# A hand-searched order of a quad's work, replaced by two orders in turn, with one more stretch in which GpSimd gets no weight steps

## Chip, cores and metric

The kernel runs on one core of a Trainium2 chip. The metric is device time in microseconds (us). Three runs of the kernel before gave 2235.53, 2234.50 and 2234.67 us, median 2234.67 us. A difference is told in us and as a share of that median.

## What is computed

A transformer block over x of 2048 tokens by 576 features, in float32: a layer norm with scale and shift, attention with 32 query heads of width 18 and one shared key and value head, the output projection added to x, a second layer norm pair, and an MLP of width 4608 with GELU, added to x.

```python
mod = (_silu(c) @ w_mod).reshape(c.shape[0], 6, 1, -1)
sa, ca, ga, sb, cb, gb = (mod[:, 0], mod[:, 1], mod[:, 2], mod[:, 3], mod[:, 4], mod[:, 5])
h = _layernorm(x, axis=-1) * (1 + ca) + sa
x = x + ga * _A_ref(h, A_wq, A_wk, A_wv, A_wo)      # 32 heads, one key/value head
h = _layernorm(x, axis=-1) * (1 + cb) + sb
x = x + gb * _B_ref(h, B_w1, B_b1, B_w2, B_b2)      # layer norm, dense, GELU, dense
```

In the attention each query row has the maximum of its scores subtracted ahead of the exponential, so every score is computed twice: once, queries by keys, to find the maximum, and once, keys by queries, for the exponential.

## The kernel before

Time falls into three parts: projections (to about 128 us), 32 "quads" of attention (to about 1380 us), and the MLP. A **quad** is four heads for one block of 512 tokens; 8 quads make a block (`NQ`), 32 all (`NQT`). The program order is written by hand: every engine takes its instructions in the order in which the code issues them, and a helper adds the waits.

What a quad does is written as a list of short words (`order`, lines 884 to 893), which the loop at lines 980 to 1021 turns into instructions:

- `S0`, `S1` (`st_mm`, matmul L931): one score tile, 128 keys by 512 queries, into a `psB` bank of PSUM, by the upper or the lower 64 rows of TensorE (the digit); ScalarE (ACT) takes the exponential of it into `P` (L933). 64 a quad.
- `M0`, `M1` (`mx_mm`, matmul L319): one score tile, queries by keys, of the **next** quad into a `psM` bank; VectorE (DVE) takes its row maximum (L953). 48 a quad.
- `X1` and `R1`: the same for a folded pair of key blocks: `X1` is a matmul (L941) into `psB` and a Relu on ACT (L944) into `xc`, `R1` a matmul into `psM` and a fused add and maximum on DVE (L951). 8 of each.
- `V2` to `V4` (`pv_mm`, L921): so many quarters of a step P times V, into the one `psC` bank, eight quarters behind the scores. A quad has 64 quarters; a step of four is called kc, 0 to 15.
- `T1`, `RC`, `T2`, `OS`: the steps of `post_quad` (L738 to L758) for the quad before: its first step, a copy of `psC` to `O` on ACT, is issued when its last P times V is; then `T1` a transpose on DVE (L741), `RC` a reciprocal on DVE (L744) and behind it a product on GpSimd (POOL, L745), `T2` the transpose back on DVE (L747), `OS` a rounded copy `os` of `O` on ACT (L757), a difference on POOL (L758) and four DMAs on SP's queue.
- `F1`, `F2`: the maxima of the next quad are put together on DVE, turned by TensorE (PE, L357), split on ACT and DVE and sent by DMA into its query tile.
- `WO` (`wo_piece`, L723): 14 matmuls of the output projection into one `psB` bank, and the addition to x on DVE (L727). There are 24 such pieces; from quad 9 on, each quad has one.

`psM` has three banks, `psB` four, `psC` one. So PE can stand at most three tiles ahead of DVE and four ahead of ACT; when it meets a word whose bank is not free, all words behind it wait as well.

Three things ride along. Every second `WO` piece finishes a tile of 128 tokens, and its second layer norm (`ln2_tile`) is then issued step by step, one step at every second kc (`between`): statistics on DVE (L143, L147, L148), rows on POOL, and at the end five transposes by PE, a copy `yr` on ACT (L165) and one on DVE (L167), which are held back until the next `WO` (`held`). Weight steps (`prep`, a generator: `weight_parts`) prepare the MLP's weights on POOL and store them by SP's queue: from quad 4 on one or two of them at each kc but those in `quiet`, which before were the two kc ahead of the `F2` word. What is left of them is issued at kc 8 of quad 31. And `load_q` loads a query tile per quad.

Quads 0 to 8 use the list `QUAD`; quads 9 to 30, which hold an output piece, used `QUADW`; quad 31 has its own.

Of the kernel before, what the change touches and what calls it, by code (L numbers as in the profile page):

```python
# [19 lines left out]
NQ = H // 4  # L20
# [12 lines left out]
def block_kernel(ctx: ExitStack, tc, x, wqkv, wo, w1, b1, w2, b2, c, wmod, ident_in, out):  # L33
# [50 lines left out]
    V = pa.tile([128, S // 128, 32], F32, name="V")  # L84
# [409 lines left out]
    WO, YR, ATT, B2 = {}, {}, {}, {}  # L494
# [283 lines left out]
    def load_w1(i, what):  # L778
        for w in what.split():
            a = 4 * OPS.index(w) if w in OPS else 28  # L780
            b = min(a + 4, 31)
            sy.dma_start(W1["r"][:, a:b].bitcast(F32), w1scr[i, :, a:b])
# [86 lines left out]
    def tail_parts(o, tail, d, e=po):  # L869

        e.tensor_tensor(d, tail[:, 0], tail[:, 1], op=ALU.subtract)
        for x, y in ((o[:, :2], tail), (o[:, 2], d)):
# [11 lines left out]
    QUAD = """S0 M0 S1 S1 M0 V3 S0 M1 S1 M0 M1 S0 V3 M0 S1 M1 S0 V2 M0 S1 S1 M0 X1 S0 V4 T1 X1 M0 M1 M0 S1 S0  # L884
# [1 line left out]
            M1 V3 M0 S1 S1 M0 S0 R1 S0 V3 R1 S0 S1 M1 S0 M0 X1 V3 M0 S1 M0 S1 S0 S0 R1 V3 M0 X1 S0 M1 S0 M1  # L886
            V3 S1 M0 M0 S1 T2 S0 S1 V4 M0 S1 S0 M1 S0 M1 V3 S0 R1 S1 M0 F1 S1 S0 V3 X1 M0 S1 M0 R1 S0 F2 OS
            V4 M0 M1 S0 S1 M0 X1 V4 S1 M0 S1 S0 M1 M0 S1 V2 R1 S0 M1 S0 V2 S0 S1 M0 M1 V2 S1""".split()
    QUADW = """S0 M1 S0 S1 M0 S1 V4 M0 S1 M0 S1 S0 M1 V4 X1 M0 M1 S0 T1 X1 S0 V4 S0 M1 M0 S1 M0 S1 V4 S1 S0 RC
            R1 M0 S1 S0 R1 V4 S1 M0 S1 S0 M0 X1 M0 V3 S0 M1 S1 M0 S1 M0 S1 V3 S0 M1 S0 X1 M0 T2 OS V2 M0 R1  # L890
            S0 S1 S0 M1 WO X1 M0 S1 M0 R1 S0 V4 S1 M0 S1 M0 S1 M0 S1 V3 M1 S0 S0 M1 S0 S1 M0 V3 S0 M1 R1 S0
            S1 M0 V3 S0 M1 M1 S0 X1 S0 V3 M1 M0 S0 S1 R1 S0 V4 M0 S1 M0 F1 S0 S1 M0 S1 V4 F2 S1 M0 X1 M0 S1
            M0 V2 S1 S0 M1 S0 V2 M1 S0 S1 M0 V2 M0 S1 M0 S1 S1 S0 M1 V3 M0 X1 S0 R1 S0 R1 V3""".split()
    LASTW = "S0 S1 S0 S1 S0 S1 WO V4 S0 S1 V4".split()
    LAST = "S0 S1 S0 S1 V4 S0 S1 S0 S1 V4".split()
    P, PVt = {}, {}
# [17 lines left out]
    def pv_mm(n, kc, h0, h1):  # L914

        if kc == 0 and h0 == 0:
            PVt[n] = psC()
        t = P.pop((n, kc)) if h1 == 4 else P[n, kc]
        cs = slice(128 * h0, 128 * h1)
        for j in range(4):  # L920
            pe.matmul(PVt[n][32 * j:32 * (j + 1), cs], V[:, kc, :], t[:, j, cs],  # L921
                      start=(kc == 0 and h0 == 0), stop=(kc == 15), skip_group_check=True)
        if kc == 15 and h1 == 4:
            posts.append(post_quad(n, PVt.pop(n)))
            next(posts[0])

    def st_mm(n, kc, g, i, ps):
        if (n, kc) not in P:
            P[n, kc] = pb.tile([128, 4, TB], F32, name="P", bufs=4)
        t = ps()  # L930
        pe.matmul(t, KS[64 * g:64 * g + 64, 128 * kc:128 * (kc + 1)], QST[n][64 * g:64 * g + 64, i, :],  # L931
                  start=True, stop=True)
        ac.activation(P[n, kc][:, 2 * i + g, :], t, AF.Exp, scale=SCALE)  # L933
# [3 lines left out]
    def mx_mm(n, u, kb, what, g):  # L937
        p, qt = UNITS[u]
        if what == "X":
            t = psB()  # L940
            pe.matmul(t, QST[n][64 * g:64 * g + 64, p, 128 * qt:128 * (qt + 1)], KD1[64 * g:64 * g + 64, :],  # L941
                      start=True, stop=True)
            XC.append(pb.tile([128, 512], F32, name="xc", bufs=2))
            ac.activation(XC[-1], t, AF.Relu)  # L944
            return
        t = psM()
        o = mx_tile(n)[:, 8 * g + 4 * p + qt, (2 if what == "R" else kb):][:, :1]
        smax_mm(n, t, g, p, qt, 3 if what == "R" else kb)
        if what == "R":
            c = XC.popleft()  # L950
            ve.tensor_tensor_reduce(c, t, c, 1.0, -3.0e38, ALU.add, ALU.max, o)  # L951
        else:
            ve.tensor_reduce(o, t, axis=AX.X, op=ALU.max)  # L953

    def between(n, kc):

        if kc == 1 and n >= 1 and n + 2 < NQT:
            load_q(n + 2)
        if kc % 2 and (held[0] != "T" or not pieces):
            held[0] = step(fill)  # L960
        if n > 3 and kc not in quiet:
            for _ in range(1 + (kc % 4 != 3)):
                step(prep)
        if kc == 8 and n == NQT - 1:
            while prep:
                step(prep)
# [3 lines left out]
    def wo_next(ps):  # L970
        tb, t, h2 = pieces.popleft()
        wo_piece(tb, t, h2, ps())
        for _ in range(2):
            if held[0] == "T":
                held[0] = step(fill)
        if h2 and tb < 2:
            fill.append(ln2_rows(tb, t))

    pq = 0
    for n in range(NQT):  # L980
        ns = [0, 0]
        if n < NQT - 1:
            order = QUADW if n > NQ else QUAD
            if n == NQT - 2:
                order = order + ["WO"]
        else:
            order = []
            for d in range(8):
                order += LASTW + ["RW"] if d == 4 else LAST
                order += {1: ["T1"], 2: ["RC"], 4: ["T2"], 5: ["OS", "V4"]}.get(d, [])  # L990
        if n < NQT - 1:
            kc = sum(int(tok[1]) for tok in order[:order.index("F2")] if tok[0] == "V") // 4
            quiet = kc - 2, kc - 1
        for tok in order:
            if tok[0] == "V":
                g = int(tok[1])
                while g:
                    i = min(g, 4 - pq % 4)
                    if pq >= LAG:
                        pv_mm(*divmod((pq - LAG) // 4, 16), pq % 4, pq % 4 + i)  # L1000
                    pq, g = pq + i, g - i
                    if pq % 4 == 0:
                        between(*divmod(pq // 4 - 1, 16))
            elif tok[0] == "S":
                g = int(tok[1])
                st_mm(n, ns[g] // 2, g, ns[g] % 2, psM if ns[g] % 2 and (n == NQT - 1 or n == NQT - 2 and ns[g] > 24) else psB)
                ns[g] += 1
            elif tok in maxima:
                unit = next(maxima[tok], None)
                if unit:  # L1010
                    mx_mm(*unit, tok[0], int(tok[1]))
            elif tok == "WO":
                wo_next(psB)
            elif tok == "RW":
                for i, w in enumerate("hl"):
                    sy.dma_start(WO[w][:, KD - 1, :].bitcast(F32), woscr[i])
            elif tok[0] == "F":
                (smax_fin1 if tok == "F1" else smax_fin2)(n + 1)
            elif n:
                if next(posts[0], 0) == 0:  # L1020
                    posts.pop()
        if n == NQT - 1:
            W1["r"] = per.tile([128, 40, 128], F32R, name="w1a", tag="big", bufs=3)
            load_w1(0, " ".join(OPS) + " tails")
# [480 lines left out]
```

## Time and profile before

| what | value |
|---|---|
| median of three runs | 2234.67 us |
| the profiled execution's own time | 2233.75 us |
| its span from first to last instruction | 2232.0 us |
| so outside the span | 1.75 us |
| busy: PE, DVE, ACT, POOL | 2206.7, 1936.0, 1645.7, 1529.3 us |
| from quad 9's second kc to the start of quad 30 | 508.11 to 1304.12 us |

The profile is of one execution. An engine's busy time is the union of its instructions' times; an instruction whose start is earlier than its forerunner's end overlaps it, so that 48 reduces of 682 ns each take 30.5 us together. Where a row ends in square brackets, the engine stood idle for that long ahead of it, and the name is what it waited for last. A quad's start is taken here as the start of its first exponential. Line numbers are those of the kernel before; in the changed kernel, lines from 894 on stand five further down.

### The profile page before, as it was taken

How to read it: one execution, taken by the hardware profiler on the slowest of the kernel's cores; microseconds unless marked ns; L12 is line 12 of the kernel's file. 1: busy time of each engine (PE TensorE's matmuls, PEld its weight loads, DVE VectorE, ACT ScalarE, POOL GpSimd, SP SyncE). 2: the span in 40 equal slices, each digit the busy share in tenths (PEclk: the TensorE clock that was granted, in tenths of full speed). 3: DMA queues.
4: the chain of work that ended last, by engine and by line, in shares of the span. 5: the costliest groups of instructions: out<-in, count | busy, mean ns of one | idle time of the engine just before them, and what ended most of it. 6: DMA issues, size and time to landing. Idle time of an engine off the chain costs nothing.

```text
span 2232.0 us, 45861 instructions
## 1 busy us (share of the span) xinstructions
PE 2206.7 (99%) x16454; PEld 1437.8 (64%) x16454; DVE 1936.0 (87%) x3415; ACT 1645.7 (74%) x3145; POOL 1529.3 (69%) x1761
## 2 busy tenths in 40 slices
PE   7999999999999999999999999999999999999999
PEld 5654444444444445444454445888888898988898
DVE  7589999999999999999999982887888878888887
ACT  5579999999999999999999997444444544343443
POOL 6653456777877787778776200888888867877776
PEclk9999999999999999999999999999999999999999
DMA  6232143443433333333333101655665646676563
GB/s 232 84 129 92 34 138 121 150 135 116 145 118 123 124 135 112 124 132 121 129 124 128 44 13 60 200 179 176 180 179 175 189 126 182 182 216 189 177 185 123
DMA packets 184776, 307.99 MB, mean 138 GB/s; under 512 B 19711, under 2 KB 75407, under 8 KB 184549
## 3 DMA queue, kind: packets, MB, share of 16 engines
q1 hardware_dynamic: 184405, 304.91, 43.0%
q8 instruction: 130, 2.13, 0.4%
q14 instruction: 97, 0.79, 0.1%
q10 hardware_dynamic: 144, 0.15, 0.0%
HBM read 200.97 MB, written 93.79 MB: 132 GB/s over the span
## 4 chain that ended last, share of the span: by engine, by line
PE 88%; DVE 3%; ACT 3%; issue 1%; POOL 0%; ACTq 0%; POOLq 0%; DVEq 0%
PE psC L921 22%; PE psB L1144 18%; PE psA L1247 16%; PE psB L931 14%; PE psM L319 11%; PE psB L723 2%; ACT P L933 2%; PE psB L941 2%; PE psA L1281 1%; DVE mx L953 1%; PE psA L723 1%; DVE xc L951 1%; PE psB L155 0%; PE psB L357 0%; PE psB L248 0%
## 5 line engine op out<-in xcount | busy, mean ns | idle before, releaser
L933 ACT ACTIVATE P<-psB 128x512 f32<-128x512 f32 x2008 | 1043.6, 617 | 32.3 <-PE psM L319 10.4
L953 DVE TENSOR_REDUCE mx<-psM 128x1 f32<-128x512 f32 x1476 | 938.2, 683 | 36.2 <-PE psM L319 16.5
L319 PE MATMUL psM<-KS,qst 64*128 64x512 f32 x1722 | 601.8, 442 | 0.3 <-DVE mx L337 0.2
L931 PE MATMUL psB<-qst,KS 64*128 64x512 f32 x2008 | 586.0, 430 | 0.3 <-ACT P L933 0.2
L921 PE MATMUL psC<-P,V 128*32 128x256 f32 (+3 forms) x6424 | 575.8, 448 | 0.5 <-ACT O L738 0.5
L931 PEld LDWEIGHTS psB<-qst,KS 64*128 64x128 f32 x2008 | 303.9, 185 | 216.0 <-ACT P L933 140.4
L1144 PE MATMUL psB<-ops,w1a 128*128 128x512 f32 x1512 | 393.9, 396 | 0.2 <-DVE h L1159 0.2
L319 PEld LDWEIGHTS psM<-KS,qst 64*128 64x128 f32 x1722 | 275.6, 184 | 163.2 <-DVE mx L953 121.3
L1144 PEld LDWEIGHTS psB<-ops,w1a 128*128 128x128 f32 x1512 | 270.2, 188 | 46.8 <-DVE h L1159 0.6
L921 PEld LDWEIGHTS psC<-P,V 128*32 128x32 f32 x6424 | 140.2, 108 | 200.5 <-issue 173.3
L1253 DVE TENSOR_TENSOR XT<-psA,XT 128x576 f32<-128x576 f32 x330 | 241.8, 753 | 18.5 <-PE psA L1247 13.2
L1247 PEld LDWEIGHTS psA<-w2s,big 128*128 128x128 f32 x1584 | 223.0, 188 | 14.0 <-POOL big L1221 2.5
L1247 PE MATMUL psA<-w2s,big 128*128 128x288 f32 x1584 | 230.5, 294 | 0.0
L1157 ACT ACTIVATE psB<-gs 128x512 f32<-128x512 f32 x144 | 86.7, 602 | 127.8 <-DVE gs L1156 127.8
L1221 POOL TENSOR_TENSOR big<-s,big 128x512 fp32r<-128x512 f32 x132 | 171.1, 1296 | 10.6
L1153 ACT ACTIVATE h<-psB,b1t 128x512 f32<-128x512 f32 x144 | 98.1, 681 | 102.4 <-PE psB L1144 81.4
L951 DVE CUSTOM_DVE_ANT_0 xc<-psM,xc 128x512 f32<-128x512 f32 x246 | 165.9, 681 | 4.2 <-PE psM L319 1.9
L758 POOL TENSOR_TENSOR os<-O,os 128x512 fp32r<-128x512 f32 x31 | 40.0, 1289 | 172.2 <-ACT os L757 172.2
L944 ACT ACTIVATE xc<-psB 128x512 f32<-128x512 f32 x246 | 152.4, 620 | 5.1 <-PE psM L319 2.7
L1156 DVE SCALAR_TENSOR_TENSOR gs<-psB,h 128x512 f32<-128x512 f32 x144 | 98.6, 684 | 39.9 <-ACT psB L1154 39.8
L792 POOL TENSOR_TENSOR r<-r,r 128x256 fp32r<-128x256 f32 (+1 forms) x162 | 122.1, 754 | 13.0
L1162 ACT ACTIVATE big<-h 128x512 fp32r<-128x512 f32 x39 | 24.7, 634 | 133.8 <-DVE h L1159 133.8
(212 smaller groups left out, 3326.7 us busy)
## 6 DMA issues: line engine op xcount, KB each, us to landing
w1a<-w1scr SPq DMA_DIRECT2D x252, 256.0 KB
w2s<-w2sum SPq DMA_DIRECT2D x132, 288.0 KB
w1scr<-r SPq DMA_DIRECT2D x126, 256.0 KB
w2s<-w2scr SPq DMA_DIRECT2D x76, 288.0 KB
w2scr<-r SPq DMA_DIRECT2D x72, 288.0 KB
w2sum<-r SPq DMA_DIRECT2D x72, 288.0 KB
qst<-qscr SPq DMA_DIRECT2D x192, 72.0 KB
w1a<-w2scr SPq DMA_DIRECT2D x33, 288.0 KB
```

Of the source, the lines that this page charges most:

```text
L319: pe.matmul(o, QST[n][64 * g:64 * g + 64, p, 128 * qt:128 * (qt + 1)], KS[64 * g:64 * g + 64, 512 * kb:512 * (kb + 1)], start=True, stop=True)
L792: po.tensor_tensor(o[:, n:2 * n], src, o[:, :n].bitcast(F32), op=ALU.subtract)
L921: pe.matmul(PVt[n][32 * j:32 * (j + 1), cs], V[:, kc, :], t[:, j, cs], start=(kc == 0 and h0 == 0), stop=(kc == 15), skip_group_check=True)
L931: pe.matmul(t, KS[64 * g:64 * g + 64, 128 * kc:128 * (kc + 1)], QST[n][64 * g:64 * g + 64, i, :], start=True, stop=True)
L933: ac.activation(P[n, kc][:, 2 * i + g, :], t, AF.Exp, scale=SCALE)
L944: ac.activation(XC[-1], t, AF.Relu)
L951: ve.tensor_tensor_reduce(c, t, c, 1.0, -3.0e38, ALU.add, ALU.max, o)
L953: ve.tensor_reduce(o, t, axis=AX.X, op=ALU.max)
L1144: pe.matmul(o, x, y, start=(first and i == 0), stop=(i == len(terms) - 1), skip_group_check=True)
L1221: po.tensor_tensor(unit(u, 1), x, unit(u, 0).bitcast(F32), op=ALU.subtract)
L1247: pe.matmul(p[:, i, :288], x[:, ts_], W2S[k][:, y], start=(bool(first) and q == 0), stop=(q == 2), skip_group_check=True)
L1253: ve.tensor_tensor(o, p[:, :, :288], o, op=ALU.add)
```

## The change

`QUADW` gets new words in a new order, and a second list `QUADV` of the same kind is added. Quads 10, 12 to 30 use `QUADV`, quads 9, 11 to 29 the new `QUADW`. Both hold the same work as the list before, in 19 runs of P times V in the place of 20. `quiet` gets a third kc, the one ahead of `RC`, in all quads from 4 to 30; the two ahead of `F2` stay as a rule. Of the lists only their first lines are shown.

```diff
-    QUADW = """S0 M1 S0 S1 M0 S1 V4 M0 S1 M0 S1 S0 M1 V4 X1 M0 M1 S0 T1 X1 S0 V4 S0 M1 M0 S1 M0 S1 V4 S1 S0 RC
...
+    QUADV = """M1 M0 S1 S0 M0 S1 S1 V4 M0 X1 M0 S1 S0 M1 V4 R1 S0 S1 S0 M1 S0 V4 T1 M1 M0 S1 S0 M1 S0 V4 S1 RC
...
+    QUADW = """M0 S1 S0 M1 S0 S1 M0 V4 M1 S0 S1 S0 M1 M0 V4 M0 S1 M1 S0 S1 S0 V4 T1 S0 M1 S0 M1 M0 S1 V2 M0 S1
...
-            order = QUADW if n > NQ else QUAD
+            order = (QUADW if n % 2 else QUADV) if n > NQ else QUAD
...
-            kc = sum(int(tok[1]) for tok in order[:order.index("F2")] if tok[0] == "V") // 4
-            quiet = kc - 2, kc - 1
+            kf, kr = (sum(int(tok[1]) for tok in order[:order.index(a)] if tok[0] == "V") // 4 for a in ("F2", "RC"))
+            quiet = kf - 2, kf - 1, kr - 1
```

Three places show what moves. The first is ACT in quad 20 (a `QUADV` quad after the change) from ahead of the output piece to behind it; `os` is the copy of the attention output, `yr` the copy of the norm's transposes, which stand right behind the output piece. Before:

```order
L944 ACTIVATE xc<-psB 128x512
L757 ACTIVATE os<-O 128x512
L933 ACTIVATE P<-psB 128x512 x3
L165 ACTIVATE yr<-psB 128x4x128
L944 ACTIVATE xc<-psB 128x512
```

and of the change:

```order
L949 ACTIVATE xc<-psB 128x512 x2
L938 ACTIVATE P<-psB 128x512 x5
L757 ACTIVATE os<-O 128x512
L938 ACTIVATE P<-psB 128x512
L165 ACTIVATE yr<-psB 128x4x128
```

`os` has moved to the other side of two exponentials: one exponential instead of three stands between it and the piece.

The second place is DVE at the same piece; L727 is the addition of the piece to x, L747 the transpose `T2`, which `os` reads. Before:

```order
L953 TENSOR_REDUCE mx_13550<-psM 128x1 x8
L747 STREAM_TRANSPOSE O<-T 128x512
L953 TENSOR_REDUCE mx_13550<-psM 128x1
L951 ISA xc,mx_13550<-psM,xc 128x512
L951 ISA mx_13550 128x1
L953 TENSOR_REDUCE mx_13550<-psM 128x1
L727 TENSOR_TENSOR XT<-psB,XT 128x288
```

and of the change:

```order
L958 TENSOR_REDUCE mx_13558<-psM 128x1
L747 STREAM_TRANSPOSE O<-T 128x512
L956 ISA xc,mx_13558<-psM,xc 128x512
L956 ISA mx_13558 128x1
L958 TENSOR_REDUCE mx_13558<-psM 128x1
L727 TENSOR_TENSOR XT<-psB,XT 128x288
```

Two tiles instead of three now stand between the transpose and the addition.

The third place is ACT in quad 21 (a new `QUADW` quad) and the start of quad 22. Before, `os` stood ahead of the piece here too. Of the change, from the split of the maxima (`ms`) on:

```order
L359 ACTIVATE ms<-psB 16x128
L938 ACTIVATE P<-psB 128x512 x10
L757 ACTIVATE os<-O 128x512
L938 ACTIVATE P<-psB 128x512 x8
L949 ACTIVATE xc<-psB 128x512
L938 ACTIVATE P<-psB 128x512 x2
L738 ACTIVATE O<-psC 128x512
```

`os` has moved from the middle of the quad to its last run of words, eleven tiles ahead of the copy that writes `O` anew.

More of the change, by code (lines that the diff above doesn't have):

```diff
@@ L888, in block_kernel @@
             V4 M0 M1 S0 S1 M0 X1 V4 S1 M0 S1 S0 M1 M0 S1 V2 R1 S0 M1 S0 V2 S0 S1 M0 M1 V2 S1""".split()
-    QUADW = """S0 M1 S0 S1 M0 S1 V4 M0 S1 M0 S1 S0 M1 V4 X1 M0 M1 S0 T1 X1 S0 V4 S0 M1 M0 S1 M0 S1 V4 S1 S0 RC
[L890 to L893, printed above, removed]
+    QUADV = """M1 M0 S1 S0 M0 S1 S1 V4 M0 X1 M0 S1 S0 M1 V4 R1 S0 S1 S0 M1 S0 V4 T1 M1 M0 S1 S0 M1 S0 V4 S1 RC
+            M0 S0 S1 M0 M0 X1 V3 M1 S0 S1 S0 R1 X1 M0 V3 S1 M0 S0 S1 M1 S0 R1 V3 M0 S1 S1 S0 M0 M0 X1 V3 M1
+            X1 S0 S1 M0 R1 S0 V4 M0 S1 T2 S0 R1 OS M0 S1 WO S1 M0 M1 S0 M0 S1 S0 V3 M0 S1 M1 S1 S0 M0 X1 V3
+            M0 S1 S0 S0 R1 M0 S1 V4 M1 S0 M1 S0 S1 M0 V2 S1 M0 S1 S0 V2 S0 F1 M1 S0 M1 S1 M0 V4 F2 S0 S1 M0
+            M1 S0 M1 V4 S1 M0 S1 S0 X1 M0 V4 M0 S1 X1 M0 S0 R1 V3 M0 S1 S0 S0 R1 S1 M0 V3""".split()
+    QUADW = """M0 S1 S0 M1 S0 S1 M0 V4 M1 S0 S1 S0 M1 M0 V4 M0 S1 M1 S0 S1 S0 V4 T1 S0 M1 S0 M1 M0 S1 V2 M0 S1
+            X1 M0 S1 V3 M0 S1 M0 S1 S0 R1 X1 V3 S0 M1 S1 M0 S1 S1 M0 V3 R1 M0 S1 S0 X1 M0 X1 V4 RC S1 S0 R1
+            M0 R1 S0 WO S0 M1 M0 M0 S1 S0 X1 V3 S0 M1 S1 R1 S0 M0 X1 V3 M0 S1 S0 S0 M1 R1 S0 V3 M0 S1 S0 S0
+            M1 M0 S1 V2 M0 S1 X1 M0 V2 M1 S0 M0 S1 S0 X1 M0 V4 S1 F1 M0 S1 S0 R1 S0 M1 V4 T2 F2 S1 M0 S1 M0
+            M1 S0 V4 S0 S1 M0 S1 S0 M1 V4 S1 M0 S0 R1 S1 M0 V4 OS M0 S1 M0 S1 S0 M1 S0 V4""".split()
     LASTW = "S0 S1 S0 S1 S0 S1 WO V4 S0 S1 V4".split()
```

## Prediction

> **What bounds the kernel now.** First the page: the span, the busy shares, the slices of DVE and ACT, and the chain that ended last.
>
> ```profile
> span 2232.0 us, 45861 instructions
> PE 2206.7 (99%) x16454; PEld 1437.8 (64%) x16454; DVE 1936.0 (87%) x3415; ACT 1645.7 (74%) x3145; POOL 1529.3 (69%) x1761
> DVE  7589999999999999999999982887888878888887
> ACT  5579999999999999999999997444444544343443
> PE 88%; DVE 3%; ACT 3%; issue 1%; POOL 0%; ACTq 0%; POOLq 0%; DVEq 0%
> ```
>
> By the page PE is busy 99% and holds the chain. But the page says itself that matmul ends are modelled, and in slices 4 to 23, the quads, DVE and ACT stand at nine tenths as well. So the next view is the busy time of each engine in single quads: 5 (no output piece), 11, 20 and 21 (output piece and norm), and 29 (output piece, the norm is over).
>
> ```profile
> core 0: us, PE busy (x) PEld busy (x) DVE busy (x) ACT busy (x) POOL busy (x), PEclk, DMA share, GB/s
> 319.03:356.38 37.35, 37.35 (x365) 18.48 (x365) 36.51 (x71) 36.97 (x76) 26.83 (x40) 1.00 0.42 141
> 588.40:629.07 40.67, 40.31 (x348) 19.54 (x349) 38.80 (x78) 38.62 (x78) 31.00 (x43) 1.00 0.34 113
> 907.44:947.59 40.15, 39.79 (x342) 19.32 (x341) 38.28 (x76) 38.13 (x76) 30.57 (x42) 1.00 0.30 102
> 947.59:987.18 39.59, 39.50 (x337) 18.67 (x336) 37.93 (x75) 37.56 (x76) 31.76 (x46) 1.00 0.42 138
> 1264.99:1304.10 39.11, 39.02 (x337) 18.64 (x337) 37.27 (x72) 37.51 (x75) 3.02 (x3) 1.00 0.07 20
> ```
>
> Subtract the busy time from the length. In quad 5 DVE is idle 0.84 us and ACT 0.38: that order runs at the speed of ACT. In quad 20 DVE is idle 1.87 and ACT 2.02, in 21 it is 1.66 and 2.03, in 29 it is 1.84 and 1.60. No engine is full there: these 1.6 to 2.0 us per quad, in 22 quads, are all that an order can win. The granted clock is 1.00 everywhere. DVE is idle as long in quad 29, with POOL at 3.02 us, as in quad 21, with POOL at 31.76, so POOL's load as such isn't the limit.
>
> Where do the gaps lie? DVE in quad 20, at its start and around the output piece:
>
> ```profile
> 907.49 1.28 DVE L953 TENSOR_REDUCE mx<-psM 128x1 f32<-128x512 f32 x2
> 909.33 3.22 DVE L953 TENSOR_REDUCE mx<-psM 128x1 f32<-128x512 f32 x5 [0.56 <-PE psB L931]
> ...
> 922.22 0.70 DVE L747 STREAM_TRANSPOSE O<-T 128x512 f32<-128x512 f32 x1
> ...
> 924.03 0.68 DVE L953 TENSOR_REDUCE mx<-psM 128x1 f32<-128x512 f32 x1
> 924.98 0.46 DVE L727 TENSOR_TENSOR XT<-psB,XT 128x288 f32<-128x288 f32 x1 [0.26 <-PE psB L723]
> 925.53 0.29 DVE L167 COPY yr<-psB 128x128 f32<-128x128 f32 x1
> 925.98 1.29 DVE L953 TENSOR_REDUCE mx<-psM 128x1 f32<-128x512 f32 x2 [0.16 <-PE psM L319]
> ```
>
> Then ACT around the piece in quad 20, and in quad 21:
>
> ```profile
> 922.96 0.63 ACT L757 ACTIVATE os<-O 128x512 fp32r<-128x512 f32 x1 [0.34 <-DVE O L747]
> 923.50 1.55 ACT L933 ACTIVATE P<-psB 128x512 f32<-128x512 f32 x3
> 925.42 0.60 ACT L165 ACTIVATE yr<-psB 128x512 f32<-128x512 f32 x1 [0.36 <-PE psB L155]
> ...
> 927.84 1.57 ACT L933 ACTIVATE P<-psB 128x512 f32<-128x512 f32 x3 [0.31 <-PE psM L319]
> ```
>
> ```profile
> 963.60 0.63 ACT L757 ACTIVATE os<-O 128x512 fp32r<-128x512 f32 x1 [0.80 <-DVE O L747]
> ...
> 966.02 0.60 ACT L944 ACTIVATE xc<-psB 128x512 f32<-128x512 f32 x1 [0.33 <-PE psB L941]
> ```
>
> And PE there:
>
> ```profile
> 921.34 0.64 PE L921 MATMUL psC<-P,V 128*32 128x256 f32 x8
> 921.91 0.50 PE L319 MATMUL psM<-KS,qst 64*128 64x512 f32 x2
> ...
> 922.80 2.14 PE L723 MATMUL psB<-wos,big 126*128 126x288 f32 x14
> 924.78 0.71 PE L155 MATMUL psB<-ident,Z 128*128 128x128 f32 x5
> ...
> 926.31 1.06 PE L921 MATMUL psC<-P,V 128*32 128x512 f32 x8
> 927.31 0.49 PE L931 MATMUL psB<-qst,KS 64*128 64x512 f32 x1
> ```
>
> The output piece holds PE from 922.80 to 924.78, 1.98 us, in which no score tile comes; with the transposes it is 2.62 us, to 925.42 by ACT's row of `yr`. DVE takes 0.60 us a tile (two take 1.28, one 0.68) and may hold three: 1.8 us, less than the gap. ACT takes 0.52 a tile (1.55 / 3), and three, since the piece has the fourth bank: 1.6 us. What else stands in their queues there, `T2` (0.70) on DVE and `os` (0.63) on ACT, is what bridges it.
>
> **The change, part by part.**
>
> *Output piece in QUADV quads (10, 12 to 30: 11).* `T2` and `os` now stand behind the first of the last tiles ahead of the piece. On DVE there are then up to three tiles and `T2`, 1.8 + 0.7 = 2.5 us, against 1.98: the 0.26 at L727 goes, and most of the 0.16 behind it. On ACT up to three tiles and `os`, 1.6 + 0.6 = 2.2: the 0.31 behind the piece goes, and of the 0.34 at `os` a part, as `T2` has one tile more behind it on DVE and one exponential more on ACT. The 0.36 at `yr` stays, since the transposes stay behind the piece. That is 0.42 on DVE and about 0.5 on ACT. The gap of 0.56 at the start arises where six words with two maxima stand ahead of a run of four quarters (1.00 us of PE, 926.31 to 927.31); such a window, `R1 S0 S1 S0 M1 S0 V4`, is now third in the quad, ahead of `T1`, with two windows of three and two DVE tiles ahead of it instead of a run of `R1`. I take a third of the 0.56 as won. DVE then gains 0.6, ACT 0.5; the period can fall only by what both have lost, so **0.5 us** a quad, 5.5 us in 11. Bounds: idle time as in quad 5 (0.84 on DVE) makes it 38.28 + 0.84 = 39.12, a gain of 1.0; below nothing, a new 0.56 per quad.
>
> *QUADW quads (9 to 29: 11).* `os` leaves the piece and goes to the end, far behind its `T2`: the 0.80 (0.34 in a quad without norm) goes from ACT. But the piece now has neither `T2` nor `os` ahead of it, only `RC`, three DVE tiles and three ACT tiles: DVE's 0.26 stays, and ACT's 0.33 and 0.31 may grow to 1.98 + 0.33 - 1.6 = 0.7 together, as now. ACT wins up to 0.8, DVE only what the first window gives back, again a third of 0.56. So **0.2 us** a quad, 2.2 us. Bounds: 38.77 by quad 5's idle time, a gain of 0.8; a loss of 0.5 to 1.3, worked out with the slower rival.
>
> *GpSimd ahead of the reciprocal.* One stall in the trace is POOL's: here are DVE's and ACT's waits from 507 to 1304 us.
>
> ```profile
> DVE XT L727 <- PE psB L723: 4.8, 19, 0.3
> ...
> DVE O L747 <- POOL T L745: 1.2, 1, 1.2
> ACT os L757 <- DVE O L747: 11.8, 20, 2.1
> ```
>
> It is in quad 11, which takes 40.67 us where 21 takes 39.59. The new list has 21 quarters between `RC` and `T2` (12.8 us at 39.1 / 64 a quarter) where there were nine, `QUADV` has 16, and the weight steps of the kc ahead are gone: the product comes in time. **1.0 us**, once; nothing if it were another cause.
>
> *Weight steps left out.* There are 614: 34 for each of 18 groups, and two. A quad has room for 28 (two at a kc, one at each fourth) and issued 25 for the quiet ones; now 24 with QUAD and QUADV, 23 with QUADW. So they end at the start of quad 30 instead of late in 28. POOL has room there (3.02 us in quad 29), and the DMAs that they issue on SP's queue go with them; nothing waits. **0.** Without that room, up to 47 steps would fall on quad 31.
>
> *One P-times-V run less.* Runs of two quarters take 0.57 us (921.34 to 921.91), of four 1.00, so 0.14 of each is fixed, 0.14 x 22 = 3.1 us in all on PE. PE has room: six score tiles take 0.89 us (921.91 to 922.80), so 128 take 19.0 at most; 64 quarters, at 0.43 for two, 13.8; 20 runs 2.8; the piece 2.0. That is 37.6 of 39.6 us. **0**, at best part of 3.1. The Trainium skill, TensorEngine Tiling (Array Packing), § Tiling Modes, says that changing the tiling mode drains TensorE, which agrees with the fixed 0.14; if PE were the bound, the sum would be lower by those 3.1 us.
>
> *Late `os`.* The page's group of POOL's difference, and how often POOL waited for `os` from 508 to 1304 us:
>
> ```profile
> L758 POOL TENSOR_TENSOR os<-O,os 128x512 fp32r<-128x512 f32 x31 | 40.0, 1289 | 172.2 <-ACT os L757 172.2
> ```
>
> ```profile
> POOL os L758 <- ACT os L757: 48.6, 13, 7.3
> ```
>
> In QUADW quads there are now 12 quarters, 7.3 us, from `os` to the next copy into `O`, which must not come ahead of that difference. `os` and the difference take 0.6 + 1.3, so POOL may be 5.4 us late; in 13 of some 21 quads it wasn't late at all. **0**. Quad 11's lag bounds it: there POOL was 1.2 us more late than nine quarters (5.5 us), less its own product; 1.3 us for ACT in such a quad.
>
> Sum: 1.0 + 5.5 + 2.2 = **8.7 us**. From the profiled execution's own 2233.75 that is 2225.05; the median of the runs is 0.92 above that execution, so 2226.0.
>
> **Rivals.**
>
> *The gaps only move (same).* Both engines are nearly full, so what a window gives to DVE it takes from ACT, and 19 new windows have gaps of their own. For it: the 0.56 appears at one kind of window, and each new list holds as many windows of two DVE tiles and four ACT tiles as the old one (two). Then quad 11's 1.0 remains: 2233.7. The Trainium skill, Perfetto Trace Analysis, § Identifying the Most-Contended Engine, says that consistent bubbles can mean too little SBUF or PSUM for the next tile; by that, the order would leave them, as the banks stay three and four. Quad 5's idle 0.38 on ACT with the same banks speaks against it.
>
> *Slower: ACT overload over the end of QUADW.* Its last window, `OS M0 S1 M0 S1 S0 M1 S0 V4`, gives ACT 0.6 + 4 x 0.52 = 2.7 us against PE's seven tiles and four quarters, 1.0 + 1.0, and QUADV's first gives four exponentials again, then the copy of `O`. If ACT is already four tiles behind there, PE stands at an `S`, the `M` behind it aren't issued, and DVE starves: 0.7 in that window, and 0.56 in the window third after it, 1.3 us per pair of quads and more. At 1.3 for each of 11 pairs, 14 us, against the 8.7 won: 5.6 slower, 2240. It decides if ACT's standing excess there is over two tiles (1.0 us).
>
> *All gaps close.* Idle time as in quad 5: 1.0 and 0.8 a quad, 22 us with quad 11: 2213. For it: the list of quads 1 to 8 got there.
>
> *The stall in quad 11 stays*, as the norm's POOL steps, not the weight steps, are ahead of the product: the forecast less 1.0, 2227.
>
> **Chances.** Forecast 2220 to 2230, the stall's case in it: 0.46. All gaps close (2212 to 2220): 0.12. Same: 0.22. Slower: 0.20. So faster by over 0.2% (4.5 us, about what a measurement of this kernel can tell from no change) 0.58, within 0.22, slower 0.20. The range of 8 in 10 reaches from 2212 to 2240; the likeliest case's own is 2220 to 2230.
>
> **What would show it.** Quads in turn of about 39.6 and 39.3 us, with norm; no wait of L732 (the old L727) for the piece in even quads, and one in odd ones; ACT's wait for `T2` ahead of `os` near 0.3 in even quads and none in odd; no DVE wait for POOL's product; POOL busy into quad 29. Wrong: odd quads above 40 us with DVE gaps of 0.5 or more at the start of even quads (the slower rival), or new gaps of the same sum elsewhere (same).

## The result and the profile after

The changed kernel takes **2228.63 us** (median of 9 runs, 2227.07 to 2231.48), the kernel before 2234.50 us (9 runs). The ratio is 0.9974, with a 95% interval of 0.9965 to 0.9983: 5.9 us or 0.26% faster. The profiled execution took 2228.63 us; its span is 2226.8 us, 5.2 less than before.

The page of the changed kernel, its span, the busy shares and the chain that ended last:

```profile
span 2226.8 us, 46144 instructions
PE 2206.0 (99%) x16630; PEld 1450.2 (65%) x16630; DVE 1934.7 (87%) x3415; ACT 1642.0 (74%) x3145; POOL 1526.9 (69%) x1761
PE 95%; ACT 1%; DVE 1%; DMA 1%; POOL 1%; issue 1%; SPq 0%; ACTq 0%; POOLq 0%; DVEq 0%
```

PE's share of the chain has risen from 88 to 95%. A run below (shorter pieces) shows that PE's work alone still doesn't set the length of a quad. Single quads again, by engine: 20 (QUADV), 21 and 11 (QUADW), then 28 (QUADV) and 29 (QUADW), in which the norm is over:

```profile
core 0: us, PE busy (x) PEld busy (x) DVE busy (x) ACT busy (x) POOL busy (x), PEclk, DMA share, GB/s
905.05:944.59 39.54, 39.54 (x364) 20.47 (x363) 38.01 (x76) 38.02 (x76) 25.11 (x38) 1.00 0.43 140
944.59:984.24 39.65, 39.63 (x331) 18.77 (x329) 38.09 (x75) 37.37 (x76) 36.20 (x47) 1.00 0.31 107
548.48:588.14 39.66, 39.63 (x331) 18.77 (x329) 38.09 (x75) 37.36 (x76) 37.38 (x49) 1.00 0.34 120
1221.62:1260.59 38.97, 38.97 (x359) 19.78 (x358) 36.98 (x72) 37.48 (x75) 26.60 (x40) 1.00 0.39 128
1260.59:1299.98 39.39, 39.39 (x331) 18.64 (x329) 37.40 (x72) 37.29 (x76) 20.11 (x31) 1.00 0.25 90
```

Quad 20 has gone from 40.15 to 39.54 us, quad 11 from 40.67 to 39.66, quad 21 from 39.59 to 39.65, quad 29 from 39.11 to 39.39. Summed by the starts of the quads: the 11 even quads are 6.5 us shorter, quad 11 is 1.0 shorter, the other ten odd quads are 1.0 longer. Quad 9 starts 1.3 us later. Of that, 1.2 stand already at the start of quad 4, ahead of the first weight step that the change moves; in the other kernels of this study quad 9 starts at 468.5 to 472.6 us, so this is the spread of what comes ahead.

At the output piece, first ACT in quad 20, then in quad 21:

```profile
923.89 0.63 ACT L757 ACTIVATE os<-O 128x512 fp32r<-128x512 f32 x1 [0.22 <-DVE O L747]
924.42 0.58 ACT L938 ACTIVATE P<-psB 128x512 f32<-128x512 f32 x1
925.51 0.60 ACT L165 ACTIVATE yr<-psB 128x512 f32<-128x512 f32 x1 [0.51 <-PE psB L155]
926.05 3.54 ACT L938 ACTIVATE P<-psB 128x512 f32<-128x512 f32 x7
```

```profile
959.72 1.61 ACT L938 ACTIVATE P<-psB 128x512 f32<-128x512 f32 x3
962.66 1.58 ACT L938 ACTIVATE P<-psB 128x512 f32<-128x512 f32 x3 [1.34 <-PE psM L319]
```

In the even quad the gap of 0.31 behind the piece is gone, and the one at `os` is 0.22 instead of 0.34; the one at `yr` is 0.51 instead of 0.36. In the odd quad the wait for `T2` (0.80) is gone, and a gap of 1.34 stands behind the piece. DVE's waits from 508 to 1300 us, all that are listed (quads 10 to 29; in the table ahead of the prediction, 508.11 is the start of quad 10 and not quad 9's second kc):

```profile
DVE mx L958 <- PE psM L319: 10.1, 38, 0.4
DVE mx L958 <- PE psB L936: 7.3, 26, 0.5
DVE XT L727 <- PE psB L723: 2.7, 10, 0.3
DVE mx L958 <- PE psB L946: 1.6, 7, 0.2
DVE xc L956 <- PE psM L319: 1.5, 7, 0.4
DVE ms L360 <- ACT ms L359: 0.5, 2, 0.2
```

The wait for the piece (L727) has halved, 4.8 to 2.7 us: it is left in the ten odd quads. The wait for POOL's product isn't there any more. The split of the maxima (L360) waited 3.1 us before and 0.5 now, since in QUADW `T2`, in QUADV a norm statistic, now stands ahead of it. The waits for score tiles (L958, L956) are as long in sum as before: 20.5 against 19.9 us.

### The profile page after: what moved, and what is told of

Same layout as the page of the kernel before. It is cut to its first block, busy times and chain, and to the rows that moved or that the text cites. A ratio compares the mean times of both kernels' runs of the same rounds, so it can differ in the third digit from the quotient of the medians.

```text
span 2226.8 us, 46144 instructions
## 1 busy us (share of the span) xinstructions
PE 2206.0 (99%) x16630; PEld 1450.2 (65%) x16630; DVE 1934.7 (87%) x3415; ACT 1642.0 (74%) x3145; POOL 1526.9 (69%) x1761
## 3 DMA queue, kind: packets, MB, share of 16 engines
q8 instruction: 132, 2.16, 0.4%
## 4 chain that ended last, share of the span: by engine, by line
PE 95%; ACT 1%; DVE 1%; DMA 1%; POOL 1%; issue 1%; SPq 0%; ACTq 0%; POOLq 0%; DVEq 0%
PE psC L926 24%; PE psB L1149 18%; PE psA L1252 16%; PE psB L936 13%; PE psM L319 13%; PE psB L723 2%; PE psB L248 2%; PE psB L946 2%; PE psA L1286 1%; PE psA L319 1%; ACT P L938 1%; PE psA L723 1%; PE psB L155 1%; DMA bigw<-in_wqkv 1%; DVE mx L344 0%
## 5 line engine op out<-in xcount | busy, mean ns | idle before, releaser
L958 DVE TENSOR_REDUCE mx<-psM 128x1 f32<-128x512 f32 x1476 | 936.1, 683 | 35.9 <-PE psM L319 15.8
L319 PEld LDWEIGHTS psM<-KS,qst 64*128 64x128 f32 x1722 | 280.9, 184 | 222.4 <-DVE mx L958 147.1
L936 PEld LDWEIGHTS psB<-qst,KS 64*128 64x128 f32 x2008 | 297.0, 184 | 165.6 <-ACT P L938 111.7
L926 PEld LDWEIGHTS psC<-P,V 128*32 128x32 f32 x6600 | 148.1, 108 | 201.2 <-issue 166.5
L956 DVE CUSTOM_DVE_ANT_0 xc<-psM,xc 128x512 f32<-128x512 f32 x246 | 167.8, 682 | 5.6 <-PE psM L319 1.8
```

The lines of the kernel that those rows point to most:

```text
L319: pe.matmul(o, QST[n][64 * g:64 * g + 64, p, 128 * qt:128 * (qt + 1)], KS[64 * g:64 * g + 64, 512 * kb:512 * (kb + 1)], start=True, stop=True)
```

## Experiments

### Which list holds the gain

One line is changed, which picks the list:

```diff
-            order = (QUADW if n % 2 else QUADV) if n > NQ else QUAD
+            order = QUADV if n > NQ else QUAD      # e1_v_all
+            order = QUADW if n > NQ else QUAD      # e2_w_all
```

> QUADV in all quads from 9 to 30, QUADW in none. Theory (the gain is QUADV's alone: T2 and os ahead of the output piece bridge it, while QUADW, with 39.65 us in a quad where the old list took 39.6, gives nothing): odd quads fall from 39.65 to about 39.2 us (between QUADV's 38.97 without norm and 39.54 with the transposes), 5 us in all, 2224 us. Rival A (one run of P times V less, the same in both lists): as the change, 2228.6 us. Rival B (the two lists work only as a pair): slower than the change, 2230 us or more.

> The new QUADW in all quads from 9 to 30, QUADV in none. Theory: even quads have the unbridged piece and the transposes as well, about 40.3 us instead of 39.54, 11 quads, so 8 us more than the change: 2237 us, no faster than before. Rival A (one run of P times V less): as the change, 2228.6 us. Rival B: slower than the change by some us, without a price.

QUADV everywhere took **2229.51 us** (ratio to before 0.9975, 0.9966 to 0.9984), QUADW everywhere **2244.41** (1.0042, 1.0030 to 1.0055). Quads 20 and 21 with QUADV everywhere, then 13, 20 and 21 with QUADW everywhere:

```profile
904.71:944.59 39.88, 39.88 (x366) 20.51 (x367) 38.20 (x76) 38.22 (x77) 21.01 (x33) 1.00 0.32 105
944.59:984.02 39.43, 39.43 (x361) 19.66 (x362) 37.66 (x75) 37.78 (x75) 37.02 (x48) 1.00 0.40 132
```

```profile
628.40:671.12 42.72, 40.85 (x330) 18.68 (x327) 38.10 (x75) 37.51 (x76) 31.67 (x44) 0.96 0.34 119
915.85:956.25 40.40, 40.38 (x334) 19.49 (x332) 38.29 (x76) 37.90 (x77) 26.30 (x36) 1.00 0.30 99
956.25:995.88 39.63, 39.27 (x329) 18.68 (x327) 37.78 (x75) 37.23 (x76) 33.02 (x47) 1.00 0.39 133
```

Rival A falls as it was put: both lists have 19 runs of P times V, and they differ by 15 us. That doesn't price the run, since QUADW everywhere has losses of its own; e5 below says more, with 19 runs in both lists and nothing of the gain. QUADV carries nearly all of the gain without QUADW, but the expected 2224 was missed: odd quads did fall, to 39.43, but even ones rose to 39.88: QUADV takes longer behind QUADV than behind QUADW. A pair takes 79.31 us, against 79.19 with the change and 79.74 before. The medians of e1 and of the change are 0.9 us apart, which the intervals don't tell from nothing, so rival B isn't settled by the time.

QUADW everywhere was 7 us worse than expected. By the starts of the quads, the even ones are 7.9 us longer in sum than with the change, about as forecast; the odd ones are 9.8 longer, and there ACT's waits say why:

```profile
ACT O L738 <- POOL os L758: 10.8, 8, 1.9
```

The copy into `O` waits for POOL's difference of the late `os`. All eight waits stand early in an odd quad: POOL has the norm's step at the end of the even quad before it, and so comes late to that difference. That is the mechanism which the prediction had called "late `os`" and priced at nothing.

### The quiet stretch alone, and the lists alone

```diff
             quiet = kf - 2, kf - 1, kr - 1      # added to the old list: e3_quiet_only
-            quiet = kf - 2, kf - 1, kr - 1
+            quiet = kf - 2, kf - 1              # taken from the change: e4_orders_only
```

> The old list in all quads from 9 on, with the new rule alone: no weight steps at the kc ahead of RC. Theory: only the one stall of quad 11 goes, 1.0 us: 2233.5 us, no change that can be told. Rival C (the gain is POOL's: the weight steps delayed the product in many quads): most of the 5.9 us, 2229 us.

> The two new lists without the new rule: the weight steps ahead of RC are issued as before. Theory: between RC and T2 lie 16 and 21 quarters, 9.8 and 12.8 us, so the product is in time anyway: 2228.6 us, within 1 us. Rival C (the rule carries the gain): 2233 us or more.

The old list with the quiet stretch took **2233.13 us** (0.9993, 0.9984 to 1.0002), the new lists without it **2227.89** (0.9969, 0.9958 to 0.9981). Quad 11 of the first:

```profile
548.42:588.02 39.60, 39.50 (x337) 18.66 (x336) 37.91 (x75) 37.56 (x76) 36.07 (x52) 1.00 0.39 132
```

The stall of quad 11 is gone, 40.67 to 39.60 us, and no other quad moved. With the new lists the quiet stretch does nothing that shows: without it quad 11 takes 39.65 us all the same, and DVE waits for no product of POOL's: between `RC` and `T2` the new lists have 16 and 21 quarters, the list of before 10. Rival C falls.

### T2 and `os` at the piece

Three runs move these two words. In e5 they leave the piece in QUADV; in e6 they come to it in QUADW, with `RC` moved ahead so that they can; in e10 they come closer to it in the list of before.

```diff
-M0 S1 T2 S0 R1 OS M0 S1 WO S1 M0 M1 S0 M0 S1 S0 V3 M0 S1 M1 S1 S0 M0 X1 V3          # QUADV
+M0 S1 S0 R1 M0 S1 WO S1 M0 M1 S0 M0 S1 S0 V3 M0 S1 T2 M1 S1 S0 OS M0 X1 V3          # e5_os_behind
...
-M1 M0 S1 V2 M0 S1 X1 ... X1 V4 RC S1 S0 R1 M0 R1 S0 WO ... V4 T2 F2 ... V4 OS M0 S1    # QUADW
+M1 M0 S1 V2 RC M0 S1 X1 ... X1 V4 S1 S0 T2 R1 M0 R1 S0 OS WO ... V4 F2 ... V4 M0 S1    # e6_w_os_ahead
...
-S0 M1 S0 X1 M0 T2 OS V2 M0 R1 S0 S1 S0 M1 WO                                        # before
+S0 M1 S0 X1 M0 V2 M0 T2 R1 S0 S1 S0 M1 OS WO                                        # e10_old_bridged
```

> The change, but in QUADV the words T2 and OS are moved from ahead of the output piece to the second and third run of words behind it. Theory (T2 on DVE and os on ACT bridge the 2 us in which the piece holds PE): in even quads DVE waits 0.26 us for the piece again, ACT's gap behind it grows to 1 us or more, and a quad takes 0.5 us longer, 11 quads: 2234 us. Rival D (the gain lies in the other windows of the new lists or in the one run of P times V less; it doesn't matter where T2 and os stand): 2228.6 us within 1.5.

> The change, but the new QUADW gets what QUADV has: RC earlier (ahead of the fifth run), T2 behind two words and OS as the last word ahead of the output piece, instead of T2 and OS late in the quad. Theory: ACT's gap of 1.34 us behind the piece and DVE's 0.27 go in odd quads; DVE has 1.57 us of idle time there, and a quad falls by about 0.4 us, 11 quads: 2224 us. Rival D: 2228.6 us within 1.5. Rival E (T2 and os are missed where they stood, since each bridged a gap there): 2228 to 2232 us with the gaps moved to the end of the odd quads.

> The list of before in all quads from 9 on, with two words moved and nothing else: T2 and OS from ahead of the last run of P times V to among the words right ahead of the output piece. Theory (T2 and os next to the piece are worth half a us in any list): 22 quads, 11 us, 2224 us, and DVE's wait of 0.26 us and ACT's of 0.31 are gone. Rival H (they help only where the list around them leaves both engines a backlog; in the new QUADW the same edit gave nothing): 2234 us within 1.5, with the gaps elsewhere.

e5 took **2235.83 us** (1.0003, 0.9994 to 1.0012), e6 **2229.78** (0.9981, 0.9973 to 0.9990), e10 **2233.74** (0.9997, 0.9988 to 1.0006). Quads 20 and 21 of e5, of e6 and of e10:

```profile
910.90:950.98 40.08, 39.97 (x365) 20.54 (x363) 37.92 (x76) 37.89 (x77) 25.11 (x38) 1.00 0.41 138
950.98:990.63 39.65, 39.63 (x331) 18.76 (x329) 38.08 (x75) 37.35 (x76) 36.18 (x47) 1.00 0.31 107
```

```profile
907.15:946.73 39.58, 39.58 (x365) 20.34 (x362) 38.01 (x76) 38.03 (x77) 23.93 (x37) 1.00 0.40 133
946.73:986.39 39.66, 39.65 (x331) 18.82 (x329) 37.92 (x75) 37.50 (x76) 37.19 (x48) 1.00 0.34 117
```

```profile
908.20:948.37 40.17, 39.78 (x342) 19.30 (x341) 38.39 (x76) 38.14 (x76) 30.56 (x42) 1.00 0.30 102
948.37:987.96 39.59, 39.50 (x337) 18.68 (x336) 37.92 (x75) 37.54 (x76) 31.68 (x46) 1.00 0.42 138
```

In QUADV the two words are worth 0.54 us a quad (39.54 to 40.08), 5.7 in the even quads, and without them next to nothing is left of the change's gain. (Another 1.6 us of e5's profile is one stall in quad 11, in which PE waits 1.4 for the DMA of a query tile.) In QUADW they are worth nothing: 39.65 and 39.66 in quad 21. There DVE's wait for the piece went from 2.7 to 0.5 us, and its wait at the split of the maxima, which `T2` had covered, came back, from 0.5 to 3.2; twice, in quads 11 and 17, DVE also waited for POOL's product, 1.7 us in all. That is rival E. In the list of before they were worth nothing either (rival H), though the waits moved as expected. These are waits of ACT and of DVE in e10:

```profile
ACT xc L944 <- PE psB L941: 5.4, 6, 1.0
...
ACT xc L944 <- PE psM L319: 4.3, 6, 0.9
...
ACT os L757 <- DVE O L747: 0.3, 1, 0.3
```

```profile
DVE XT L727 <- PE psB L723: 1.6, 7, 0.2
```

ACT's 11.8 us at `os` became 9.7 at the tile behind the piece, where it had waited 3.7 before. A likely reason stands in the rows of before, and the prediction overlooked it: `os` ran at 922.96, and the piece had PE from 922.80 to 924.78. The old list's `os` was already done during the piece; what was moved towards it didn't add to the backlog. The rows above agree. Length less busy time is what an engine is idle: in quad 20 of e5 it is 2.16 us for DVE and 2.19 for ACT, with the change 1.53 and 1.52, so both lose 0.6. In e10 it is 1.78 and 2.03, where before it was 1.87 and 2.02: ACT loses nothing. Why the words give both engines something in QUADV alone isn't shown.

One more run moved them within QUADV's run of words:

```diff
-V4 M0 S1 T2 S0 R1 OS M0 S1 WO
+V4 T2 M0 S1 S0 R1 M0 S1 OS WO      # e11_t2_first
```

> The change, with two words of QUADV moved within their run: T2 to its front, into the gap of 0.27 us in which DVE waits for PE's run of P times V, and OS to its end, right ahead of the piece, so that it needn't wait for T2. Theory: ACT's 0.22 us at os and DVE's 0.27 go, DVE's wait for the piece comes back by 0.1 or so: 0.1 to 0.3 us in 11 quads, 2226 to 2227.5 us. Rival (the gaps only move): 2228.6 us.

**2227.99 us** (0.9973, 0.9961 to 0.9984), and even quads as with the change (quad 20: 39.56). The wait at `os` went, and DVE's wait for the piece came back in all 20 quads, 6.6 us in sum instead of 2.7. The rival holds: the gaps moved.

### Which list in which quad

```diff
-            order = (QUADW if n % 2 else QUADV) if n > NQ else QUAD
+            order = (QUADV if n % 2 else QUADW) if n > NQ else QUAD      # e7_swapped
```

e8 keeps the rule and puts the list of before in QUADW's place; e12 is e8 with two words of that list moved to where QUADW has them.

```diff
-X1 M0 T2 OS V2 M0 R1 ... V4 F2 S1 ... V3 M0 X1 S0 R1 S0 R1 V3      # the old list, e8_v_and_old
+X1 M0 V2 M0 R1 ... V4 T2 F2 S1 ... V3 OS M0 X1 S0 R1 S0 R1 V3      # e12_old_wide
```

> The two new lists with their parity swapped: QUADV in odd quads, QUADW in even ones. Theory (the late os of QUADW fits only quads in which GpSimd isn't behind): the norm's big step falls on GpSimd in the even quads at kc 13, os's difference comes 5 to 6 us late there as with QUADW in all quads, the next copy into O waits 1 to 2 us, and the transposes stand behind an unbridged piece: 2235 to 2240 us. Rival (which of the two comes in which quad doesn't matter): 2228.6 us within 1.5.

> QUADV in even quads, the list of before in odd ones, and the new rule. Theory (the gain is QUADV's in even quads; the new QUADW is no better than the old list): 2228 to 2229 us, as the change. Rival B (the two lists fit each other at their seams): even quads at 39.9 instead of 39.5 us, as QUADV behind QUADV has, and 2232 us.

> QUADV in even quads and the old list in odd ones, as in the run before that gave 2241.3 us, but in the old list T2 and OS stand late, T2 ahead of F2 and OS ahead of the last run, as in the new QUADW; the rest of the old list is as it was. There T2 waited 6.8 us for GpSimd's product, and os 14.6 us for T2. Theory (what the new QUADW does for QUADV is the wide room between RC and T2, since QUADV's later output piece moves the norm's GpSimd step to a later kc and so GpSimd's lag into the odd quads): both waits go and the odd quads fall from 40.16 and more to about 39.7 us, 2230 us or a little less. Rival (the other windows of QUADW are needed at the seams as well): the waits go, but odd quads stay at 40 us or above, 2235 us or more.

e7 took **2250.15 us** (1.0074, 1.0060 to 1.0088), e8 **2241.30** (1.0031, 1.0019 to 1.0042), e12 **2235.11** (1.0006, 0.9997 to 1.0015). In all three the theory missed. Quads 17 and 20 of e7; 20, 21 and 25 of e8; 20 and 21 of e12:

```profile
795.12:838.41 43.29, 40.84 (x359) 19.87 (x358) 38.06 (x75) 37.77 (x75) 34.09 (x48) 0.96 0.43 137
919.71:960.30 40.59, 40.57 (x336) 19.67 (x334) 38.47 (x76) 37.90 (x78) 22.78 (x31) 1.00 0.27 94
```

```profile
910.77:950.53 39.76, 39.76 (x365) 20.60 (x365) 38.01 (x75) 38.12 (x77) 20.97 (x33) 1.00 0.32 106
950.53:994.23 43.70, 41.75 (x339) 19.61 (x336) 38.23 (x76) 37.65 (x76) 38.04 (x50) 0.96 0.39 135
1113.94:1154.10 40.16, 40.07 (x339) 18.96 (x336) 38.10 (x76) 37.77 (x76) 37.81 (x49) 1.00 0.36 120
```

```profile
909.51:949.30 39.79, 39.79 (x365) 20.67 (x365) 38.02 (x75) 38.14 (x77) 22.57 (x35) 1.00 0.36 113
949.30:989.53 40.23, 40.14 (x339) 19.06 (x336) 37.89 (x76) 37.66 (x77) 35.68 (x47) 1.00 0.37 127
```

What GpSimd did, in one wait of e7 and two of e8:

```profile
ACT O L738 <- POOL os L758: 11.0, 6, 3.8
```

```profile
DVE O L747 <- POOL T L745: 6.8, 4, 2.5
```

```profile
ACT os L757 <- DVE O L747: 14.6, 20, 3.2
```

e7 is the late `os` again, now with 3.8 us at worst, and again the even quads are longer as well. e8 refutes "the new QUADW is no better than the old list": beside QUADV the old list stalls on POOL's product, in quads 11, 13, 17 and 21. QUADV's output piece stands behind 32 quarters, the old list's behind 28, and a step of the norm comes with the kc that ends at 32. So with QUADV a norm tile starts one step, two kc, later, and POOL's rows of the norm come later in its queue too. POOL before, from the norm's first row to the product behind the next `RC`, and then POOL of the change, from the norm's statistic, which POOL waits for, to the same row:

```profile
938.72 2.30 POOL L585 TENSOR_SCALAR Z<-XT,mv,rs 128x576 f32<-128x576 f32 x1
...
955.78 1.05 POOL L745 TENSOR_TENSOR T<-T,R 128x512 f32<-128x512 f32 x1 [1.76 <-DVE R L744]
```

```profile
941.10 0.23 POOL L149 TENSOR_SCALAR rs<-mv 128x1 f32<-128x1 f32 x1 [11.65 <-DVE mv L148]
...
945.11 2.30 POOL L585 TENSOR_SCALAR Z<-XT,mv,rs 128x576 f32<-128x576 f32 x1
```

Quad 20 starts at 907.44 before and at 905.05 in the change, so the norm's rows start 31.3 us into it before and 40.1 us now, half a us into quad 21. In e12 the room between `RC` and `T2` is wide, and DVE's wait for POOL is gone, and with it the quads of 41 to 44 us. But odd quads stay at 40.2. The piece is unbridged there (DVE's wait for it is 7.9 us in sum), yet that alone doesn't explain it: quad 25 of e8, with the two words at the piece and no wait for POOL, takes 40.16 too, where the old list behind itself took 39.59 (quad 21 before). So the old list is half a us longer behind QUADV, and QUADW isn't; the rival, that QUADW's other windows are needed at the seams, holds there, but which of them it is isn't shown. QUADV too depends on what stands ahead of it: quad 20 takes 39.54 us behind QUADW, 39.76 and 39.79 behind the old list, 39.88 behind itself. So e8's rival B has a part in its loss.

### Is it PE?

```diff
-                terms = [(ah, wh), (ah, wl), (al, wh)]
+                terms = [(ah, wh), (ah, wl)] if tb < NB - 1 else [(ah, wh), (ah, wl), (al, wh)]
...
-                terms = [(ah, wh), (al[:5 * DH], wl[:5 * DH])]
+                terms = [(ah, wh)]
```

> The change, with shorter output pieces: of the first three token blocks' projection the product of the attention output's low part with the weights' high part is left out, and the low-by-low tail term, so a piece has 9 matmuls instead of 14 and holds PE 0.7 us less; the output is less exact by those terms. Theory (DVE and ACT bound the quads, and the piece costs only what isn't bridged): the bridged even quads fall by 0.3 us or less, the odd ones, with ACT's gap of 1.34 us, by about 0.5, 2220 us. Rival F (PE has become the bound: it is busy 39.54 of 39.54 us in an even quad and holds 95% of the chain): every quad falls by the full 0.7 us, 15 us, 2213 us. Rival G (ACT's gap in odd quads costs nothing): odd quads as they are, 2225 us.

**2218.95 us** (0.9930, 0.9917 to 0.9944). Quads 20, 21, 27 and 28:

```profile
899.97:939.20 39.23, 39.08 (x359) 19.66 (x358) 37.80 (x76) 38.09 (x76) 25.16 (x38) 1.00 0.44 142
939.20:978.45 39.25, 39.19 (x326) 17.93 (x324) 37.90 (x75) 37.62 (x76) 36.19 (x46) 1.00 0.31 108
1174.70:1213.62 38.92, 38.92 (x326) 17.88 (x324) 37.18 (x72) 37.46 (x77) 22.62 (x33) 1.00 0.33 113
1213.62:1252.41 38.79, 38.72 (x354) 19.00 (x353) 36.82 (x72) 37.49 (x75) 26.65 (x40) 1.00 0.39 128
```

PE's 0.7 us less per piece give 0.31 in the even quad 20, 0.40 in 21, 0.18 in 28 (QUADV) and 0.46 in 27 (QUADW; 39.38 us with the change). F falls: PE's 95% of the chain doesn't mean that a quad goes by PE's work. G falls as it was put, but the run doesn't show that ACT's gap is what costs: DVE's wait for the piece, 2.7 us in sum with the change, isn't listed any more either. The quads with the bridged piece gain less, as expected, but not nothing.

## Where the prediction held and where it failed

- **The time and its sign**: forecast 2226.0, measured 2228.63; a gain of 5.9 us where 8.7 was summed. That it came so near is in part luck: the term for QUADW had the wrong sign, and the one for QUADV was too small.
- **What bounds a quad** (DVE and ACT together, not PE): held in part. With the shorter piece a quarter to two thirds of what PE saved came through; no run shortens DVE's or ACT's own work.
- **QUADV quads, 5.5 us**: 6.5 in the profiles. e5 shows that in QUADV it hangs on `T2` and `os` at the piece. But the step that derived it took the gain from their standing nearer to the piece; in the list of before `os` ran within the piece already, and moving them nearer in that list gave nothing (e10). What QUADV's other windows do, which without the two words are as good as the old list with them, isn't settled.
- **A third of the 0.56 at the quad's start**: not shown. In every even quad from 10 on, gaps of 0.25 and 0.21 to 0.24 us took its place, in every odd one a gap of 0.22 to 0.23; yet DVE's waits for score tiles are as long in sum; what DVE gained are the waits for the piece, for POOL and for the split of the maxima, the last of which the prediction didn't see.
- **QUADW quads, 2.2 us: wrong.** They lost 1.0 us without quad 11. ACT's gap of 0.7 "as now" was 1.34. That gap alone doesn't cost it, since filling it gave nothing (e6): DVE is the fuller one there, busy 38.09 us of 39.65 against ACT's 37.37. The loss is small in each quad, and what makes it isn't settled.
- **Quad 11's stall, 1.0 us**: held in size (1.0), and e3 shows the quiet stretch able to remove it. But with the new lists the room between `RC` and `T2` does it without the stretch (e4).
- **Weight steps left out, 0**: held. POOL is busy 20.11 us in quad 29, where it was 3.02, and without the quiet stretch (e4) the time is the same.
- **One run less, 0**: no run isolates it. e5 has 19 runs in both lists and took 2235.83 us, so the run less alone isn't the gain.
- **Late `os`, 0**: held for this change only, because QUADW stands in odd quads. The step took POOL's lag from the trace of before, in which the norm's rows came 9 us earlier, and asked of no even quad. In e2 and e7, 16 and 22 us slower than the change, its wait is new; the odd quads, where it stands, hold about half of that; the even quads, with their unbridged piece, hold the rest.
- **The rival that the gaps only move** held in the QUADW quads and in e10 and e11. It didn't hold in the QUADV quads: there the order alone, with the same banks, took quad 20 from 40.15 to 39.54 us.
- **The slower rival** (ACT overloaded over QUADW's end) didn't come: the gaps at the start of even quads are 0.25 us and less.
- Slips: L727 keeps its number in the changed kernel, it isn't L732. Between `RC` and `T2` the list of before has ten quarters (16 to 26), not nine. "All gaps close" adds up to 21 us, not 22. The Trainium skill's sentence on consistent bubbles stands in § Optimization Strategy of Perfetto Trace Analysis, right behind the section named.

No run beat the change by more than the intervals tell: e4 and e11 are 0.7 and 0.6 us lower, and the shorter pieces leave terms out.

## What to carry to other kernels

Before a filler is moved towards a gap, look in the trace whether it already runs in it: the order in the program says where it stands in its queue, not when it runs. In a quad with two nearly full engines, removing a listed wait gave a gain here only where the other engine lost one too; compare the lengths of stretches, not sums of waits. And a word that moves past a step counter moves what rides on the counter: here an output piece four quarters later put GpSimd's work several us later, which one partner list could bear and another couldn't.

## What the runs showed of the hardware

Some stalls cost more than their wait, as the granted clock fell behind them. In e8's quad 21 `os` waited 3.2 us for `T2`, PE stood idle for 1.86, and then two stretches of 4 us ran at 0.75 and 0.83:

```profile
966.00:970.00 4.00, 2.42 (x17) 1.94 (x15) 1.63 (x3) 0.89 (x2) 3.78 (x7) 1.00 0.47 168
970.00:974.00 4.00, 3.72 (x18) 1.46 (x20) 3.62 (x10) 2.67 (x6) 3.85 (x6) 0.75 0.19 74
974.00:978.00 4.00, 4.00 (x38) 1.78 (x34) 3.24 (x6) 3.39 (x7) 3.76 (x8) 0.83 0.38 97
978.00:982.00 4.00, 4.00 (x44) 2.35 (x42) 3.62 (x7) 3.88 (x9) 3.81 (x4) 1.00 0.57 202
```

That is 0.25 and 0.17 of 4 us, 1.7 us of clock in all; a window from 972.0 to 975.3 us shows 0.50 throughout. A mean of 0.96 over a whole quad stands in the rows of quad 13 of e2, 17 of e7 and 21 of e8, and in no row of a quad without such a stall. The Trainium skill, TensorE: Matmul & The Clock Gate, § Part 1: The HAM clock gate, tells of half the rate after an idle window of about 3.4 us. The half rate agrees, and 1.7 us lost at half rate make the slow stretch 3.4 us long; but in PE's own rows here the idle gap ahead of it was 1.86 us, so a shorter one was enough. Nor did the length of the gap alone decide it: in e2, gaps of 1.87 and 1.79 us in PE's rows (quads 13 and 17) were followed by such a stretch, gaps of 1.83 and 1.80 (quads 19 and 23) by none.
